# Attention block of an adaLN transformer layer: score and maxima products over 128 rows, zeroed padding rows, and the maxima product ahead of its score

## The chip, the cores and the metric

The kernel runs on one core of a Trainium2 chip. That core has a matrix engine (PE, with its weight loads shown as PEld), a vector engine (DVE), an activation engine (ACT), a general engine (POOL), a queue that issues transfers (SP), an on-chip memory of 128 partitions (rows), and 8 banks of accumulator memory, each 128 x 512 float32. The metric is the device time of one execution in microseconds (us); lower is better.

## The reference, cut to what matters

The input x is 2048 x 448. The block is a layer norm with modulation, attention with 16 heads of width 28, a residual, then a second layer norm with a gated MLP. Only the attention part is touched:

```
qkv = (x @ wqkv) -> q, k, v          # per head: 2048 x 28
scores = einsum("bhqd,bhkd->bhqk", q, k) * (28 ** -0.5)
p = softmax(scores, axis=-1)
o = einsum("bhqk,bhkd->bhqd", p, v)
```

## The kernel before, in words

**Split operands.** q and k are each kept as a high part and a low remainder, so that one product of 3 x 28 = 84 rows gives high·high + high·low + low·high. For each head there is a `kst` and a `qst` tile of 128 partitions x 2048 columns; three of each exist, and head h uses number h % 3. `load_head` (L343) fills rows 0 to 83 of both by six transfers from a scratch tensor in device memory.

**Two products for each score.** The softmax needs each query's maximum before the exponentials. So every block of scores is made twice. `m_mm` (L396) makes a 128-query x 512-key block with rows 0 to 83, and DVE reduces it to row maxima (L404). When a head's maxima are complete, `m_fin` (L412) transposes them, negates them, splits them in two and writes them by two transfers into rows 84 and 85 of `qst`. `s_mm` (L427) later makes a 128-key x 512-query block with rows 0 to 85: rows 84 and 85 of `kst` hold ones, so this product subtracts the maximum, and ACT takes the exponential (L434) into a tile `P`.

**The loop.** A unit is one block of 128 keys (for scores) or of 128 queries (for maxima); there are 16 x 16 = 256 units. In unit u the loop (L572) issues four score products of unit u and four maxima products of unit u + 20, alternating, score first. After every second unit it issues the eight value products of two units (`pv_mm`, L441), each 32 columns wide, four side by side, recorded as two passes each: 16 records. I call the 16 score and maxima products and the 16 records after them a **period**. There are 116 periods that hold pairs; the last units have scores only.

**What sets the order.** The order on each engine is written out by hand. Score and maxima blocks take their bank from one pool of 7 (`bank`, L161). Which earlier block's bank a product gets, and so whose release it waits for, is fixed when the program is built. A score block's bank is released by ACT's exponential, a maxima block's by DVE's reduction. Transfers go through SP in the order in which they are written.

**Before the loop.** The first 80 maxima products stand between the matrix products of `qk_unit` (L280), which make the last q and k columns. The `kst` and `qst` tiles come into being at g == 3 (L336), ahead of the last value products (L271). There POOL writes ones into rows 64 to 85 of `kst` tiles 0 and 1 (L346), and during `qk_unit` those of tile 2 (L569).

Of the kernel before, what the change touches and what calls it, by code (L numbers as in the profile page):

```python
# [8 lines left out]
F32 = mybir.dt.float32  # L9
# [24 lines left out]
def tile_adaln_mha_gmlp(ctx, tc, x, wqkv, wo, w_in, w_spT, b_sp, w_out, cT, w_mod, out):  # L34
    nc = tc.nc
    ctx.enter_context(tc.manual_schedule())
    pe, dve, act, pool, sp = nc.tensor, nc.vector, nc.scalar, nc.gpsimd, nc.sync
# [51 lines left out]
    def weight_part(dst, i, raw, hi_eng, lo_eng, zero=True):  # L89

        n = raw.shape[-1]
        h = dst[:, i if i < 3 else 6, 0:n]
        if hi_eng is act:
            act.activation(h, raw, AF.Copy)
        else:
            hi_eng.tensor_copy(h, raw)
        if i < 3:
            sub(lo_eng, dst[:, 3 + i, 0:n], raw, h)
        else:
            sub(lo_eng, dst[0:64, 7, 0:n], raw[0:64], h[0:64])  # L100
            if zero:
                pool.memset(dst[64:128, 7, 0:n].bitcast(F32), 0.0)
# [6 lines left out]
    def ln_transpose(xns, full_pool, dsts, scol, bcol, engs, los=(pool,) * 4, mid=None, after=None):  # L109

        tps = []
        for c in range(4):
            tp = bank("tp")
            tps.append(tp)
            for t in range(4):
                pe.transpose(tp[:, t * 128 : (t + 1) * 128], xns[t][:, c * 128 : (c + 1) * 128], ident)  # L116
        if mid:
            mid()
        for c in (0, 2, 1, 3):
            tp = tps[c]  # L120
            f = full_pool.tile([128, 512], F32, name="hfull")
            if engs[c] is act:
                act.activation(f, tp, AF.Identity, scale=scol[:, c : c + 1], bias=bcol[:, c : c + 1])
            else:
                engs[c].tensor_scalar(
                    out=f, in0=tp, scalar1=scol[:, c : c + 1], scalar2=bcol[:, c : c + 1], op0=ALU.mult, op1=ALU.add
                )
            hi = dsts[:, c if c < 3 else 6, :]
            if engs[c] is act:
                act.activation(hi, f, AF.Copy)  # L130
            else:
                engs[c].tensor_copy(hi, f)
            if c < 3:
                sub(los[c], dsts[:, 3 + c, :], f, hi)
            else:
                sub(los[c], hi[64:128], f[64:128], hi[64:128])
            if after:
                after(c)
# [22 lines left out]
    def bank(name):  # L161
        return ring.tile([128, 512], F32, name=name, tag="s")

    def load_mod(pair, eng):
        for k in range(4):
            wms[pair, k] = e1.tile([112, 2, D], F32, name="wm", bufs=4)
            eng.dma_start(wms[pair, k], w_mod[:, pair, k])

    def load_x(g, eng):
        xg = e1.tile([128, 4, D], F32, name="xg")  # L170
        for t0, t1 in ((0, 1), (1, 2), (2, 4)) if g == 0 else ((0, 4),):
            eng.dma_start(xg[:, t0:t1, :], x[g, :, t0:t1])
        for t in range(4):
            xts[4 * g + t] = xg[:, t, :]
# [91 lines left out]
    def v_tiles(*kts):  # L266
        pvs = [bank("pv") for _ in kts]
        for j, (a, b) in enumerate(STEPS):
            for kt, pv in zip(kts, pvs):
                g, t = divmod(kt, 4)  # L270
                pe.matmul(pv[:, :D], hT[g][:, a, t * 128 : (t + 1) * 128], wv[:, b, :], start=j == 0, stop=j == NST - 1)  # L271
        for kt, pv in zip(kts, pvs):
            dve.tensor_copy(V[:, kt, :, 0:DH], pv[:, :D].rearrange("p (h d) -> p h d", d=DH))

    def qk_unit(m, g, mid=None):
        pq = bank("pq")
        for j, (a, b) in enumerate(STEPS):
            if mid and j in mid:
                mid[j]()
            pe.matmul(pq, wqk[:, b, m * 128 : (m + 1) * 128], hT[g][:, a, :], start=j == 0, stop=j == NST - 1)  # L280
        f = stage.tile([128, 512], F32, name="qf")
        act.activation(f, pq, AF.Copy)  # L282
        hi = stage.tile([128, 512], F32R, name="qh")
        act.activation(hi, f, AF.Copy)
        lo = stage2.tile([128, 512], F32R, name="ql")
        sub(pool, lo, f, hi)
        for i, t in enumerate((hi, lo)):
            sp.dma_start(qk_scr[i][m * 128 : (m + 1) * 128, g * 512 : (g + 1) * 512], t.bitcast(F32))
# [42 lines left out]
    for g in range(NG):  # L331
        if g + 2 < NG:
            load_x(g + 2, sp)
        if g in (0, 2):
            load_mod(1 + g // 2, sp)
        if g == 3:  # L336
            early.close()
            stk = att.enter_context(tc.tile_pool(name="stk", bufs=1))
            kq = [[stk.tile([128, S], F32R, name=f"{n}st{i}") for n in "kq"] for i in range(3)]
            kst, qst = [a[0] for a in kq], [a[1] for a in kq]  # L340
            npool = att.enter_context(tc.tile_pool(name="npool", bufs=2))

            def load_head(h, c0=0, c1=S):  # L343
                k, q = kst[h % 3], qst[h % 3]
                if h < 2 and c0 == 0:
                    pool.memset(k[64:86, :].bitcast(F32), 1.0)  # L346
                for r0, i in ((0, 0), (56, 1), (28, 0)):
                    sp.dma_start(k[r0 : r0 + 28, c0:c1].bitcast(F32), qk_scr[i][D + h * DH : D + (h + 1) * DH, c0:c1])
                for r0, i in ((0, 0), (28, 1), (56, 0)):
                    sp.dma_start(q[r0 : r0 + 28, c0:c1].bitcast(F32), qk_scr[i][h * DH : (h + 1) * DH, c0:c1])  # L350

            load_head(0, 0, 1536)
            for m in (0, 3):
                qk_unit(m, g)
            load_head(0, 1536, S)
        if g == 0:
            v_tiles(0, 1)
            v_tiles(2)
        else:
            v_tiles(4 * g)  # L360
            v_tiles(4 * g + 1)
        if g == 0:
            for i in range(4):
                weight_part(wqk, i, raws.pop(("qk", i)), act, (dve, pool)[i % 2], False)
        if g + 1 < NG:
            ln_transpose(xns, e1, hT[g + 1], cols["ca"], cols["sa"], (act,) * 4)
        if g + 2 < NG:
            ln_stats(g + 2)
            xns = ln_norm(g + 2)
        if g > 0:  # L370
            v_tiles(4 * g + 2)
        else:
            pool.memset(V[:, :, :, DH:32], 1.0)
        v_tiles(4 * g + 3)
        if g == 2:
            mod_bc("ga", accs[1][:, 0, :])
            mod_col(("sb", accs[1][:, 1, :], 0.0))
        if g < 3:
            for m in (0, 3):
                qk_unit(m, g)  # L380
        if g in (1, 2):
            for k in range(4):
                mod_acc(g, k)
# [12 lines left out]
    def m_mm(j, kb):  # L396
        h, t = divmod(j, NT)
        mt = bank("mt")
        pe.matmul(  # L399
            mt, qst[h % 3][0:84, t * 128 : (t + 1) * 128], kst[h % 3][0:84, kb * 512 : (kb + 1) * 512], start=True, stop=True  # L400
        )
        if h not in pms:
            pms[h] = npool.tile([128, NT, 4], F32, name="pm")
        dve.tensor_reduce(out=pms[h][:, t, kb : kb + 1], in_=mt, axis=AX.X, op=ALU.max)  # L404
# [22 lines left out]
    def s_mm(u, qb):  # L427
        h, kt = divmod(u, NT)
        st = bank("st_ps")
        pe.matmul(st, kst[h % 3][0:86, kt * 128 : (kt + 1) * 128], qst[h % 3][0:86, qb * 512 : (qb + 1) * 512], start=True, stop=True)  # L430
        if qb % 2 == 0:
            ptiles[u, -1] = ppool.tile([128, 2, 512], F32, name="P")
        p = ptiles[u, -1][:, qb % 2, :]
        act.activation(p, st, AF.Exp, scale=SCALE)  # L434
        ptiles[u, qb] = p
# [129 lines left out]
                        fn(*a)  # L565

    for i, (m, g) in enumerate((m, g) for m in (4, 1, 5, 2, 6) for g in range(NG)):
        if i == 4:
            pool.memset(kst[2][64:86, :].bitcast(F32), 1.0)  # L569
        qk_unit(m, g, {j: m_first for j in (1, 4, 7, 10)})  # L570

    for u in range(NU + 1):  # L572
        for fn, a in events.pop(u, []):
            fn(*a)
        j = u + LEAD
        for qb in range(4 if u < NU else 0):
            s_mm(u, qb)
            if j < NU:
                m_mm(j, qb)
        if u % 2 == 0 and u > 0:  # L580
            pv_mm(u - 2)
            pv_mm(u - 1)
        for fn, a in late.pop(u, []):
            fn(*a)
# [109 lines left out]
    h = H - 1  # L694
# [203 lines left out]
    for tb in range(NG):  # L898
        nj = 3 if tb == NG - 1 else 2
        for st in range(NT - nj):  # L900
# [8 lines left out]
            if tb > 0 and 1 <= st < 13:  # L909
                t, part = 4 * (tb - 1) + (st - 1) // 3, (st - 1) % 3  # L910
# [54 lines left out]
```

## Time and profile before

| What | Value |
|---|---|
| median of 3 runs | 1462.51 us |
| profiled execution, its own time | 1460.85 us |
| span of its instructions | 1459.1 us |
| granted clock of the matrix engine, mean | 0.997 |
| PE busy | 1436.4 us (98%) |
| DVE busy | 881.3 us (60%) |
| ACT busy | 732.4 us (50%) |
| POOL busy | 276.3 us (19%) |
| score and maxima products | 1024 each |

The profile is of one execution. A matrix product's recorded time covers its way through the array, so consecutive ones overlap, and the step from one start to the next is what a product costs. A share of busy time says little here for the same reason; the timeline, which gives starts, says more. The `x1` or `x8` at the end of a timeline line is the number of instructions that were merged into it.

### The profile page before, as it was taken

The numbers are of one execution on the slowest core, as the hardware profiler recorded it, in microseconds if no ns is written. First come the engines' busy times: TensorE is split into PE (matmuls) and PEld (weight loads), VectorE is DVE, ScalarE is ACT, GpSimd is POOL, SyncE is SP. The second block draws the span as 40 slices with busy tenths as digits, with TensorE's granted clock in tenths as the row PEclk, the third lists the DMA queues.
The fourth block names the chain that finished last, engine by engine and source line by source line (L and its number), as shares of the span: only waits on it lengthen the run. The fifth ranks groups of instructions, "written<-read, shape, count | busy, mean of one in ns | idle before, by whom it ended". The sixth has DMA issues, their size and how long they took to land.

```text
span 1459.1 us, 19621 instructions
## 1 busy us (share of the span) xinstructions
PE 1436.4 (98%) x7314; PEld 1017.5 (70%) x7314; DVE 881.3 (60%) x1458; ACT 732.4 (50%) x1390; POOL 276.3 (19%) x255
## 2 busy tenths in 40 slices
PE   6999999999999999999999999999999999999999
PEld 5887755555555555555555556888988888888887
DVE  6557888888888888888888832921542411414114
ACT  3523576777677767777776786452432211211111
POOL 6734200000002021001000022100663400302002
PEclk9999999999999999999999999999999999999999
DMA  7564401221022211222132003432003322323223
GB/s 216 149 173 152 139 11 43 53 51 42 15 52 53 53 38 42 53 51 53 32 76 53 10 19 124 155 120 94 14 23 97 121 76 67 108 64 100 84 69 108
DMA packets 56131, 111.23 MB, mean 76 GB/s; under 512 B 11900, under 2 KB 22780, under 8 KB 53516
## 3 DMA queue, kind: packets, MB, share of 16 engines
q1 hardware_dynamic: 55910, 109.81, 25.9%
q8 instruction: 57, 0.93, 0.3%
q14 instruction: 38, 0.31, 0.1%
q10 hardware_dynamic: 126, 0.17, 0.0%
HBM read 75.89 MB, written 29.48 MB: 72 GB/s over the span
## 4 chain that ended last, share of the span: by engine, by line
PE 94%; DVE 3%; DMA 2%; issue 1%; SPq 0%; ACT 0%; POOL 0%; DVEq 0%; ACTq 0%
PE st_ps L430 18%; PE mt L399 16%; PE o_ps L445 16%; PE acc L848 6%; PE acc L850 6%; PE acc L849 6%; PE pq L280 5%; PE z_ps L802 5%; PE z_ps L736 5%; PE pv L271 2%; PE y_ps L889 2%; PE y_ps L888 2%; PE y_ps L890 2%; PE tp L116 1%; PE wo_ps L618 1%
## 5 line engine op out<-in xcount | busy, mean ns | idle before, releaser
L404 DVE TENSOR_REDUCE pm<-mt 128x1 f32<-128x512 f32 x1024 | 632.3, 683 | 120.6 <-PE mt L399 120.2
L434 ACT ACTIVATE P<-st_ps 128x512 f32<-128x512 f32 x1024 | 514.4, 621 | 153.4 <-PE st_ps L430 153.0
L430 PE MATMUL st_ps<-qst,kst 86*128 86x512 f32 x1024 | 410.6, 412 | 0.0
L399 PE MATMUL mt<-kst,qst 84*128 84x512 f32 x1024 | 405.7, 396 | 0.3 <-DVE pm L404 0.3
L430 PEld LDWEIGHTS st_ps<-qst,kst 86*128 86x128 f32 x1024 | 193.1, 189 | 145.2 <-issue 82.1
L445 PE MATMUL o_ps<-P,V 128*32 128x512 f32 x2048 | 247.5, 599 | 0.0
L399 PEld LDWEIGHTS mt<-kst,qst 84*128 84x128 f32 x1024 | 195.1, 190 | 37.1 <-DVE pm L404 0.7
L83 DVE TENSOR_TENSOR wsp_l<-raw_sp,wsp_h 128x512 fp32r<-128x512 f32 x64 | 50.8, 796 | 189.4 <-ACT wsp_h L785 189.4
L785 ACT ACTIVATE wsp_h<-raw_sp 128x512 fp32r<-128x512 f32 x64 | 40.2, 631 | 232.1 <-DMA raw_sp<-in_w_spT_dram 191.1
L445 PEld LDWEIGHTS o_ps<-P,V 128*32 128x32 f32 x2048 | 54.2, 109 | 123.4 <-issue 116.1
L83 POOL TENSOR_TENSOR heapF<-u,heapD 128x512 fp32r<-128x512 f32 x27 | 44.6, 1684 | 256.8 <-ACT heapD L867 256.8
L848 PE MATMUL acc<-wsp_h,heapD 128*128 128x512 f32 x224 | 87.7, 392 | 1.3 <-DVE u L865 1.3
L850 PE MATMUL acc<-wsp_h,heapD 128*128 128x512 f32 x224 | 87.5, 390 | 0.0
L849 PE MATMUL acc<-wsp_l,heapD 128*128 128x512 f32 x224 | 87.4, 390 | 0.0
L471 POOL TENSOR_TENSOR osb<-osb,rb 128x512 f32<-128x512 f32 x15 | 19.2, 1277 | 355.3 <-DMA rb<-r_scr 263.8
L280 PE MATMUL pq<-heapD 128*128 128x512 f32 x196 | 64.6, 407 | 0.0
L83 POOL TENSOR_TENSOR nl<-nf,nh 16x128 fp32r<-16x128 f32 x16 | 7.2, 449 | 278.9 <-issue 147.5
L893 DVE TENSOR_TENSOR x2t<-x2t,y_ps 128x448 f32<-128x448 f32 x12 | 7.4, 621 | 72.9 <-PE y_ps L890 72.9
L282 ACT ACTIVATE qf<-pq 128x512 f32<-128x512 f32 x28 | 16.7, 597 | 69.0 <-PE pq L280 69.0
L848 PEld LDWEIGHTS acc<-wsp_h,heapD 128*128 128x128 f32 x224 | 42.1, 188 | 10.5 <-DVE u L865 2.3
L850 PEld LDWEIGHTS acc<-wsp_h,heapD 128*128 128x128 f32 x224 | 42.1, 188 | 8.9
L849 PEld LDWEIGHTS acc<-wsp_l,heapD 128*128 128x128 f32 x224 | 42.1, 188 | 8.2
(162 smaller groups left out, 1753.8 us busy)
## 6 DMA issues: line engine op xcount, KB each, us to landing
raw_sp<-in_w_spT_dram SPq DMA_DIRECT2D x64, 256.0 KB
kst<-qk_scr SPq DMA_DIRECT2D x45, 224.0 KB
qst<-qk_scr SPq DMA_DIRECT2D x45, 224.0 KB
qk_scr<-qh SPq DMA_DIRECT2D x28, 256.0 KB
qk_scr<-ql SPq DMA_DIRECT2D x28, 256.0 KB
z_scr<-z1t SPq DMA_DIRECT2D x28, 256.0 KB
z<-z_scr SPq DMA_DIRECT2D x28, 256.0 KB
wm<-in_w_mod_dram SPq DMA_DIRECT2D x12, 392.0 KB
```

Of the source, the lines that this page charges most:

```text
L83: eng.tensor_tensor(out=dst, in0=a, in1=hi.bitcast(F32), op=ALU.subtract)
L280: pe.matmul(pq, wqk[:, b, m * 128 : (m + 1) * 128], hT[g][:, a, :], start=j == 0, stop=j == NST - 1)
L399: pe.matmul(mt, qst[h % 3][0:84, t * 128 : (t + 1) * 128], kst[h % 3][0:84, kb * 512 : (kb + 1) * 512], start=True, stop=True)
L404: dve.tensor_reduce(out=pms[h][:, t, kb : kb + 1], in_=mt, axis=AX.X, op=ALU.max)
L430: pe.matmul(st, kst[h % 3][0:86, kt * 128 : (kt + 1) * 128], qst[h % 3][0:86, qb * 512 : (qb + 1) * 512], start=True, stop=True)
L434: act.activation(p, st, AF.Exp, scale=SCALE)
L445: pe.matmul(otile[h][32 * qb : 32 * qb + 32, :], V[:, kt, h, :], ptiles.pop((u, qb)), start=kt == 0, stop=kt == NT - 1)
L736: pe.matmul(ps_t, w1[:, b, f * 128 : (f + 1) * 128], h2T[g][:, a, :], start=j == 0, stop=j == NST - 1)
L802: pe.matmul(ps_t[:, :D], h2T[g][:, a, tt * 128 : (tt + 1) * 128], w2[:, b, hf * D : (hf + 1) * D], start=j == 0, stop=j == NST - 1)
L848: pe.matmul(acc[f], z2[st][:, 0, fs], hi, start=st == 0, stop=False)
L849: pe.matmul(acc[f], z2[st][:, 0, fs], lo, start=False, stop=False)
L850: pe.matmul(acc[f], z2[st][:, 1, fs], hi, start=False, stop=st == NT - 1)
```

## The change

The change has four parts.

- **128 rows.** `m_mm` and `s_mm` read all 128 rows of `kst` and `qst` instead of 84 and 86.
- **Zeros.** A new function `pads` writes zeros into rows 64 to 127 of each `kst` tile on DVE, zeros into rows 64 to 127 of each `qst` tile (tile 0 on DVE, tiles 1 and 2 on POOL), and then the ones into rows 64 to 85 of `kst` on POOL. Tile 0 is done where the tiles come into being, tiles 1 and 2 after two value tiles; the three former writes of ones go.
- **Clearing the old maxima.** The maxima product now also reads rows 84 and 85 of `qst`, where ones in `kst` meet them. `load_head` therefore starts with one more transfer for each head from 3 on, which copies the zeros of rows 86 and 87 over the maxima that the tile's former head left.
- **Order.** In each pair of the loop the maxima product is issued ahead of the score product.

```diff
+            def pads(i, eng):
+                dve.memset(kst[i][64:128, :].bitcast(F32), 0.0)
+                eng.memset(qst[i][64:128, :].bitcast(F32), 0.0)
+                pool.memset(kst[i][64:86, :].bitcast(F32), 1.0)
+
+            pads(0, dve)
+
             def load_head(h, c0=0, c1=S):
                 k, q = kst[h % 3], qst[h % 3]
-                if h < 2 and c0 == 0:
-                    pool.memset(k[64:86, :].bitcast(F32), 1.0)
+                if h > 2:
+                    sp.dma_start(q[84:86, :].bitcast(F32), q[86:88, :].bitcast(F32))
...
             v_tiles(4 * g)
             v_tiles(4 * g + 1)
+        if g == 3:
+            pads(1, pool)
+            pads(2, pool)
...
-            mt, qst[h % 3][0:84, t * 128 : (t + 1) * 128], kst[h % 3][0:84, kb * 512 : (kb + 1) * 512], start=True, stop=True
+            mt, qst[h % 3][:, t * 128 : (t + 1) * 128], kst[h % 3][:, kb * 512 : (kb + 1) * 512], start=True, stop=True
...
-        pe.matmul(st, kst[h % 3][0:86, kt * 128 : (kt + 1) * 128], qst[h % 3][0:86, qb * 512 : (qb + 1) * 512], start=True, stop=True)
+        pe.matmul(st, kst[h % 3][:, kt * 128 : (kt + 1) * 128], qst[h % 3][:, qb * 512 : (qb + 1) * 512], start=True, stop=True)
...
-        if i == 4:
-            pool.memset(kst[2][64:86, :].bitcast(F32), 1.0)
...
         for qb in range(4 if u < NU else 0):
-            s_mm(u, qb)
             if j < NU:
                 m_mm(j, qb)
+            s_mm(u, qb)
```

## The prediction

> **What bounds the kernel now.** I read the list of costliest groups first.
>
> ```profile
> L404 DVE TENSOR_REDUCE pm<-mt 128x1 f32<-128x512 f32 x1024 | 632.3, 683 | 120.6 <-PE mt L399 120.2
> L434 ACT ACTIVATE P<-st_ps 128x512 f32<-128x512 f32 x1024 | 514.4, 621 | 153.4 <-PE st_ps L430 153.0
> L430 PE MATMUL st_ps<-qst,kst 86*128 86x512 f32 x1024 | 410.6, 412 | 0.0
> L399 PE MATMUL mt<-kst,qst 84*128 84x512 f32 x1024 | 405.7, 396 | 0.3 <-DVE pm L404 0.3
> ```
>
> DVE and ACT both wait for PE, and PE's products hardly wait. So in the loop PE's issue steps set the time. The timeline of one period (starts in the first column) gives these steps.
>
> ```profile
> 313.68 0.19 PEld L430 LDWEIGHTS st_ps<-qst,kst 86*128 86x128 f32 x1 [0.84 <-issue]
> 313.68 0.50 PE L430 MATMUL st_ps<-qst,kst 86*128 86x512 f32 x1
> 314.02 0.40 PE L399 MATMUL mt<-kst,qst 84*128 84x512 f32 x1
> ...
> 314.22 4.04 ACT L434 ACTIVATE P<-st_ps 128x512 f32<-128x512 f32 x8 [1.69 <-PE st_ps L430]
> 314.26 0.40 PE L430 MATMUL st_ps<-qst,kst 86*128 86x512 f32 x1
> ...
> 314.46 2.48 DVE L404 TENSOR_REDUCE pm<-mt 128x1 f32<-128x512 f32 x4 [0.92 <-PE mt L399]
> ...
> 317.30 0.39 PE L399 MATMUL mt<-kst,qst 84*128 84x512 f32 x1
> ...
> 317.62 1.92 PE L445 MATMUL o_ps<-P,V 128*32 128x512 f32 x16
> ```
>
> From 314.02 to 317.30 there are 14 steps: 3.28 / 14 = 0.234 us each. The first step is 0.34, since after the value products the weight load isn't ahead; the first score really starts 0.11 after its load, at 313.79. The next period begins at 319.47, 5.79 later. Over the 116 periods with pairs the trace has 5.82 on average.
>
> ACT starts 0.43 after its first score starts. Eight activations take 4.04, the last itself about 0.65: (4.04 - 0.65) / 7 = 0.485 from start to start. DVE: (2.48 - 0.68) / 3 = 0.60. ACT's 0.485 is slower than the 0.467 in which a pair is issued, so ACT falls behind within each period and catches up during the value products, 1.69 idle before the next. This decides below.
>
> **Part 1, 128 rows.** The trace has long rows of 128-row products with the same 512 columns.
>
> ```profile
> 1201.42 0.39 PE L848 MATMUL acc<-wsp_h,heapD 128*128 128x512 f32 x1
> 1201.65 0.39 PE L849 MATMUL acc<-wsp_l,heapD 128*128 128x512 f32 x1
> 1201.87 0.39 PE L850 MATMUL acc<-wsp_h,heapD 128*128 128x512 f32 x1
> ```
> ```profile
> 995.63 10.59 PE L736 MATMUL z_ps<-heap,heapA 128*128 128x512 f32 x46
> ```
>
> (10.59 - 0.39) / 45 = 0.2267 us a step, 0.0066 below the 0.2333 of the score and maxima products. Is it the rows, or that each of these products waits for a bank and signals? In `qk_unit` before the maxima products come (74 to 84 us) the 128-row products step at 0.227, waits between units included. Once one 84-row product stands after every three or four (95 to 100 us), every step is 0.231 to 0.238, also between two 128-row products. Around 1000 us DVE or ACT at work changes nothing. So I take the rows as the cause and 0.227 for the new step. The bounds are 0.227 and 0.234; a loss I exclude, as no long run of 128-row products is slower.
>
> The Trainium skill speaks against a gain: "TensorE: Matmul & The Clock Gate", section "Why this matters for your kernels", says that a product with a small contraction takes the same time as one of 128 rows. By that the sum is rival B's; the two rates above disagree with it, though they come from different lines.
>
> Saved if nothing else changed: 15 steps x 0.0066 = 0.10 a period, x 116 = 11.5 us; in `qk_unit` 300 products (80 + 20 units x 11) x 0.0064 = 1.9; where scores stand alone (10 blocks, step 0.231) 0.3. Sum 13.7 us.
>
> **Part 2, the order.** It moves no instruction to another engine, but which bank release each product waits for changes. I took the waits from both programs as built and number a period's products 0 to 15.
>
> Before, product 14 (a score) waits in most periods for the activation of product 8, the fifth score. Counted from product 0: that activation starts at 0.43 + 4 x 0.485 = 2.37, ends 0.62 later (L434's mean) at 2.99; the load follows a release by 0.05 (a reduction that ended at 305.30 let a load start at 305.35), and the product follows its load by 0.11: 3.15. By the steps alone it is due at 14 x 0.2333 = 3.27. No wait, by 0.12.
>
> After, product 14 is a maxima product and waits for the activation of product 9, again the fifth score, but the first score now starts one step later: 0.227 + 3.15 = 3.38. By the steps it is due at 14 x 0.227 = 3.18. It waits **0.20 us**. Behind it in PE's queue stand the last score and the value products, so the whole period moves. Net of the 0.10 saved: +0.10.
>
> So it is five times in the eight periods of a head. I carried the same durations through the other three. One, where product 14 waits for an older maxima block, has no wait: -0.10. The two after a head's maxima transpose (which takes a bank from the same pool) wait already in the trace (periods of 5.94 and 5.83) and get 0.08 and 0.13 longer. Carried through the program of before, the same rows give 5.78 and 5.94, near the trace. A head: 5 x 0.10 + 0.08 + 0.13 - 0.10 = 0.61, x 14.5 heads (116 periods / 8) = **+8.8 us**.
>
> DVE gains: its first block comes one step earlier. It isn't late: eight reductions of 0.60 are 4.8 in a period of 5.8.
>
> **Part 3, zeros and ones.**
>
> ```profile
> 0.82 0.17 DVE L52 MEMSET ones<- 128x128 f32 x1 [0.82 <-PEq L953]
> 0.93 0.06 DVE L54 MEMSET mhalf<- 128x4 f32 x1
> ```
> ```profile
> 82.17 1.80 POOL L346 MEMSET kst<- 22x2048 f32 x1
> ```
>
> POOL's write of 2048 columns takes 1.80, so 1.8 for its new ones. On DVE 124 columns more cost about 0.10, so 2048 cost some 1.75. Tile 0 (two on DVE, then POOL's ones) comes at about 79 to 84 us; DVE is idle from 78.6 to 86.7 and POOL writes its ones at 82.17 anyway. Tiles 1 and 2: 3.5 on DVE between the value copies of 88.96 and 91.20, which makes two copies up to 1.9 late; seven banks cover that. On POOL four writes, 7.2, from 87.2 on; it then has nothing to do until 100.1. The head's loads on SP wait for the scratch tensor until 84.2 and, for tile 1, issue at 96.5. I take 0; with this cover gone it would be tile 0's 5.3.
>
> **Part 4, the clearing transfer.** 13 transfers of 16 KB, first of each head's loads on SP, where such an issue takes 0.38. It waits for the former head's last score, as the loads behind it do. These loads are issued ten units (29 us) before their first maxima product, and no wait in the loop names a transfer on PE. Cost 0, at most those 13 x 0.38 = 5 us on SP, hidden.
>
> **The sum.** +8.8 - 1.9 - 0.3 = +6.6 us. On the profiled execution's 1460.85 that is 1467.5; the median is 1.7 above that execution, so I forecast **1469.1**, +0.5%. About 2% is what a measurement of this kernel can tell from no change.
>
> **Rivals.**
> - B, rows are free: the step stays 0.2333. Nothing is saved, and product 14 comes at 0.233 + 3.15 = 3.38 against 3.27: +0.115. A head: 5 x 0.115 + 0.09 + 0.13 = 0.80, x 14.5 = 11.5, so 1474. For it: every score and maxima product has its own wait and signal, those at 1000 us do not. Against: the 84-row products spoil the steps of their 128-row neighbours.
> - C, the other side: the activation's release comes early enough and the rows' gain stays whole. It decides at 0.20: product 14's load would have to find its bank free at 3.18 - 0.11 = 3.07 instead of 3.27, as with steps of ACT of 0.435. For it: ACT's steps vary between 0.477 and 0.494. Against: none is that short. 1462.5 - 13.7 = 1449.
> - D, neither a gain nor a wait: 1462.5.
> - E, weight loads no longer run ahead. The first step of a period shows the price: 0.34 instead of 0.23, 0.105 for each of 15 x 116 steps, +183, so 1645. Against: at L848 to L850, with 128 rows, the steps hold no load. The Trainium skill has such a rule, "TensorE: Matmul & The Clock Gate", section "Part 3: Packing small matmuls": a load overlaps a running product only where the row groups differ; the 0.227 steps contradict it.
>
> **How the numbers follow.** My case 0.58, B 0.20, C 0.10, D 0.04, a setup that shows or waits that spread 0.07, E 0.01. My case alone holds 1465 to 1473 (ACT's step of 0.477 or 0.494 moves the wait by 0.03, 2.4 us). The range goes up to B with the setup's 5.3, 1479, and down to a release 0.15 earlier than worked out (0.15 x 5 x 14.5 = 11), 1457, which holds D; C and the slowest are left out. Faster by over 2%: 0.02, slower by over 2%: 0.04, within: 0.94.
>
> **What would show it.** Steps of 0.227 between maxima and score products in most of a period; then one long step, 0.38 to 0.43, before product 14, with the weight load of `mt` waiting for ACT's `P` (9.4 us in all before, for `st_ps`), and a period near 5.9. Steps of 0.233 throughout show B; a period near 5.7 without the long step shows C. SP and POOL should show no new wait ahead of the first maxima product at 95.2. The forecast fails if the banks are released by other times than these, or if the steps between 128-row products that each wait and signal are neither of the two rates.

## The result and the profile after

The changed kernel takes 1474.2 us (median), the kernel before 1462.3: a ratio of 1.0087, 95% interval 1.0069 to 1.0105. One execution of the kernel before, at 3635.2 us, is left out of the ratio, so the ratio is not exactly the quotient of these medians. The change makes the kernel slower by 0.7 to 1.05%: less than the 2% that the prediction names, but the whole interval lies above 1. The forecast was 1469.1, +0.5%, and the time lies inside its range of 1457 to 1479.

The profiled execution after has a span of 1474.0 us, 15.0 more than before. By the first and last products of each stage in the two timelines it divides like this:

| Stage | before | after | difference |
|---|---|---|---|
| start to the first maxima product | 95.2 | 99.5 | +4.3 |
| from there to the first score (`qk_unit` with maxima products) | 70.4 | 68.8 | -1.6 |
| first score to the last value product (the loop) | 727.2 | 740.0 | +12.8 |
| the rest | 566.2 | 565.7 | -0.5 |

The 4.3 us at the start belong to this one execution. There DVE's longest wait for input rows was 9.6 us instead of 4.4, ahead of anything the change touches. Of the kernels below with the same setup, one begins its maxima products at 94.9, and one whose DVE waited 9.7 us begins them at 99.1. The loop is where the time came from.

The list of costliest groups of the changed kernel, for the lines that answer to those shown of before:

```profile
L415 DVE TENSOR_REDUCE pm<-mt 128x1 f32<-128x512 f32 x1024 | 631.4, 680 | 132.4 <-PE mt L410 132.1
L445 ACT ACTIVATE P<-st_ps 128x512 f32<-128x512 f32 x1024 | 512.9, 629 | 169.6 <-PE st_ps L441 168.2
L410 PE MATMUL mt<-kst,qst 128*128 128x512 f32 x1024 | 424.0, 414 | 0.3 <-DVE pm L415 0.3
L441 PE MATMUL st_ps<-qst,kst 128*128 128x512 f32 x1024 | 395.1, 397 | 0.0
```

The same instructions, all with 128 rows, and both DVE and ACT sit idle for PE longer than before (132 and 170 us against 121 and 153). PE itself shows next to no idle time, because the recorded times of its products overlap: below, product 13 is still recorded as running, to 339.91, when the late load of product 14 begins at 339.83. The load shows the wait. This is one ordinary period in the timeline of the changed kernel:

```profile
336.40 0.19 PEld L410 LDWEIGHTS mt<-kst,qst 128*128 128x128 f32 x1 [0.84 <-issue]
336.40 0.50 PE L410 MATMUL mt<-kst,qst 128*128 128x512 f32 x1
...
336.73 0.39 PE L441 MATMUL st_ps<-qst,kst 128*128 128x512 f32 x1
...
337.22 4.03 ACT L445 ACTIVATE P<-st_ps 128x512 f32<-128x512 f32 x8 [1.93 <-PE st_ps L441]
...
339.28 0.39 PE L410 MATMUL mt<-kst,qst 128*128 128x512 f32 x1
...
339.51 0.40 PE L441 MATMUL st_ps<-qst,kst 128*128 128x512 f32 x1
339.83 0.19 PEld L410 LDWEIGHTS mt<-kst,qst 128*128 128x128 f32 x1 [0.30 <-ACT P L445]
339.83 0.50 PE L410 MATMUL mt<-kst,qst 128*128 128x512 f32 x1
...
340.17 0.40 PE L441 MATMUL st_ps<-qst,kst 128*128 128x512 f32 x1
...
340.49 1.92 PE L456 MATMUL o_ps<-P,V 128*32 128x512 f32 x16
...
342.35 0.50 PE L410 MATMUL mt<-kst,qst 128*128 128x512 f32 x1
```

From product 1 (336.73) to product 13 (339.51) there are 12 steps of 2.78 / 12 = 0.232 us. Then the weight load of product 14 waits for the activation and begins at 339.83. The product really starts 0.11 later, at 339.94, 0.43 after product 13, so it lost 0.20. The period lasts 342.35 - 336.40 = 5.95 us, where an ordinary one lasted 5.77 to 5.81, 5.80 on average. Over all 116 periods the mean went from 5.818 to 5.932.

The list of waits shows the same in total. Its columns are the time, the number of waits and the longest. First the largest wait of a load for ACT before, then the one after:

```profile
PEld st_ps L430 <- ACT P L434: 9.4, 39, 0.4
```
```profile
PEld mt L410 <- ACT P L445: 34.8, 98, 0.8
```

Before, a maxima product's load waited 0.7 us in all for `P`.

### The profile page after: what moved, and what is told of

The parts are those of the page before. It is cut to its first block, busy times and chain, and to the rows that moved or that the text cites. A ratio compares the mean times of both kernels' runs of the same rounds, so it can differ in the third digit from the quotient of the medians.

```text
span 1474.0 us, 19620 instructions
## 1 busy us (share of the span) xinstructions
PE 1448.4 (98%) x7314; PEld 1008.6 (68%) x7314; DVE 887.4 (60%) x1462; ACT 732.4 (50%) x1390; POOL 282.2 (19%) x257
## 4 chain that ended last, share of the span: by engine, by line
PE 92%; DMA 3%; POOL 2%; DVE 1%; issue 1%; SPq 1%; ACT 0%; DVEq 0%; ACTq 0%; POOLq 0%
PE mt L410 19%; PE st_ps L441 16%; PE o_ps L456 16%; PE acc L858 6%; PE acc L859 6%; PE acc L857 6%; PE z_ps L811 5%; PE z_ps L745 5%; PE pq L280 4%; PE wo_ps L627 2%; PE y_ps L898 2%; PE y_ps L897 2%; PE y_ps L899 2%; DMA raw_sp<-in_w_spT_dram 1%; DMA raw<-in_wqkv_dram 1%
## 5 line engine op out<-in xcount | busy, mean ns | idle before, releaser
L410 PE MATMUL mt<-kst,qst 128*128 128x512 f32 x1024 | 424.0, 414 | 0.3 <-DVE pm L415 0.3
L441 PE MATMUL st_ps<-qst,kst 128*128 128x512 f32 x1024 | 395.1, 397 | 0.0
L410 PEld LDWEIGHTS mt<-kst,qst 128*128 128x128 f32 x1024 | 192.1, 188 | 143.3 <-issue 77.3
L441 PEld LDWEIGHTS st_ps<-qst,kst 128*128 128x128 f32 x1024 | 191.6, 188 | 61.7 <-issue 7.5
```

What stands on the lines that cost most here:

```text
L410: pe.matmul(mt, qst[h % 3][:, t * 128 : (t + 1) * 128], kst[h % 3][:, kb * 512 : (kb + 1) * 512], start=True, stop=True)
L441: pe.matmul(st, kst[h % 3][:, kt * 128 : (kt + 1) * 128], qst[h % 3][:, qb * 512 : (qb + 1) * 512], start=True, stop=True)
```

## Experiments

Theory 1 is the prediction's: the new order makes product 14 wait for the bank of the fifth score, the 128 rows save a little on each step, and the setup is hidden. Theory 2 puts the loss on the 128-row products. Theory 3 puts it on the setup and the clearing transfers.

### The order alone

```diff
         for qb in range(4 if u < NU else 0):
-            s_mm(u, qb)
             if j < NU:
                 m_mm(j, qb)
+            s_mm(u, qb)
```

> Only the order of each pair is changed; the products keep 84 and 86 rows, and the writes of ones stay as before. Theory 1 (the bank of the fifth score): product 14 of a period waits for the fifth activation, 3.38 us after product 0 against 3.27 due, so about +0.11 us in five of eight periods and about as much more around a head's maxima transpose; ordinary periods of 5.89 to 5.91 us, two long steps before and after product 14, about +11 us, ratio 1.006 to 1.009. Theory 2 (the 128-row products and what fills them are the loss, the order is free): periods as before, 5.78 to 5.80, ratio 0.999 to 1.001.

Measured: 1476.4 us, ratio 1.0100 (1.0085 to 1.0115). The loop takes 740.8 us, as in the changed kernel. The timeline of its PE shows products 12, 13 and 14 of a period:

```profile
339.06 0.40 PE L399 MATMUL mt<-kst,qst 84*128 84x512 f32 x1
339.30 0.39 PE L430 MATMUL st_ps<-qst,kst 86*128 86x512 f32 x1
339.58 0.50 PE L399 MATMUL mt<-kst,qst 84*128 84x512 f32 x1
```

The load of the last of these starts with the product, at 339.58, so the product starts at 339.69, 0.39 after the one before. Ordinary periods last 5.96 us, +0.17, more than the +0.11 expected, and the ratio is above the 1.006 to 1.009 expected. The trace shows where the other 0.06 comes from: ACT takes the first score 0.49 us after its start, as in the changed kernel, and not 0.43. The whole loss is here: the order makes it, without any of the other parts.

### The rows alone

The changed kernel with the former order:

```diff
         for qb in range(4 if u < NU else 0):
+            s_mm(u, qb)
             if j < NU:
                 m_mm(j, qb)
-            s_mm(u, qb)
```

> 128 rows with the zeros and the clearing transfer, but score first as before. Theory 1: no wait at product 14; the steps fall to 0.231 for the first seven products of a period and 0.227 behind them where no load is late, so periods of 5.72 to 5.76 us instead of 5.79, and 2 us less ahead of the loop; 1453 to 1458, ratio 0.994 to 0.998. Theory 2: the loss of the whole change stays here, ratio 1.005 to 1.009. If the rows do nothing at all: ratio 0.999 to 1.001.

Measured: 1454.3 us, ratio 0.9946 (0.9932 to 0.9961). **This kernel beats both.** Ordinary periods last 5.73 us and the mean period 5.775. In the middle of a period:

```profile
323.23 0.39 PE L410 MATMUL mt<-kst,qst 128*128 128x512 f32 x1
323.46 0.39 PE L441 MATMUL st_ps<-qst,kst 128*128 128x512 f32 x1
...
324.59 0.39 PE L410 MATMUL mt<-kst,qst 128*128 128x512 f32 x1
```

Six steps lie between the first and the last of these: (324.59 - 323.23) / 6 = 0.227 a step. Theory 2 falls. But not all steps are like this. After a period's first step they run 236, 228, 232 and 231 ns, sometimes with one or two more of this kind, before they stay at 227; that is reached at the sixth or seventh product. Where a load has waited even a little, the next steps swing in the same way. The mean of the steps below 0.25 is 0.2304 here, 0.2312 in the changed kernel, and 0.2341 before.

### The setup alone

The changed kernel with the former order and with 84 and 86 rows again:

```diff
-            mt, qst[h % 3][:, ...], kst[h % 3][:, ...]
+            mt, qst[h % 3][0:84, ...], kst[h % 3][0:84, ...]
...
-        pe.matmul(st, kst[h % 3][:, ...], qst[h % 3][:, ...]
+        pe.matmul(st, kst[h % 3][0:86, ...], qst[h % 3][0:86, ...]
```

> Zeros, ones and the clearing transfer of the change, but products of 84 and 86 rows and score first. Theory 1: hidden, ratio 0.999 to 1.001, the first maxima product at 95 to 97 us, periods as before. Theory 3 (the setup or the 13 transfers hold something up): 3 to 6 us more, ratio 1.002 to 1.004, seen as a later first maxima product or as long periods where the clearing transfers are issued.

Measured: 1461.4 us, ratio 1.0002 (0.9991 to 1.0014); first maxima product at 94.9 us, mean period 5.816. Theory 3 falls: zeros, ones and the 13 transfers cost nothing that can be measured (at most 2 us, by the interval).

### Shorter activations in the changed kernel

If product 14 waits for the fifth activation, a shorter activation must take the wait away although nothing on PE changes.

```diff
-            ptiles[u, -1] = ppool.tile([128, 2, 512], F32, name="P")
+            ptiles[u, -1] = pst[(2 * u + qb // 2) % 6]    # six fixed tiles, filled with ones
...
-        act.activation(p, st, AF.Exp, scale=SCALE)
+        act.activation(p[:, 0:384], st[:, 0:384], AF.Exp, scale=SCALE)
```

> The changed kernel with shorter activations: the exponential is taken of 384 of the 512 columns of each score block; the other 128 columns of six fixed P tiles hold ones, so that part of the softmax is left out. Nothing changes on the matrix engine. Theory 1: an activation step falls from 0.485 to about 0.37 us, the fifth is over before product 14 is due, the long steps there vanish and ordinary periods fall from 5.95 to 5.74 to 5.78 us; 1452 to 1458, ratio 0.993 to 0.998. If what product 14 waits for is not the activation but a reduction or the matrix engine itself: periods stay at 5.95 us, 1470 to 1475.

Measured: 1452.0 us, ratio 0.9935 (0.9919 to 0.9951). A period in its timeline, with seven of its eight activations and the last products:

```profile
317.65 3.29 ACT L448 ACTIVATE P<-st_ps 128x384 f32<-128x384 f32 x7 [1.97 <-PE st_ps L444]
...
319.96 0.39 PE L444 MATMUL st_ps<-qst,kst 128*128 128x512 f32 x1
320.19 0.39 PE L413 MATMUL mt<-kst,qst 128*128 128x512 f32 x1
320.42 0.40 PE L444 MATMUL st_ps<-qst,kst 128*128 128x512 f32 x1
```

Products 13, 14 and 15 follow each other at 0.23. Ordinary periods fall from 5.95 to 5.73 us, as long as with the rows alone: there the order costs nothing once ACT is quicker. One part of the expectation missed. An activation lasts 0.49 us instead of 0.62, but its step falls only to (3.29 - 0.49) / 6 = 0.47, not to 0.37, since ACT now keeps up with PE and waits for each score.

The same edit with 448 columns shows how close it is:

> The changed kernel with exponentials of 448 of the 512 columns (128 of the 1024 columns of each P tile hold ones instead; that part of the softmax is left out). Theory 1: the activation's own time falls by about 0.05 us and its step below the 0.463 us of a pair, so the fifth score's bank comes free 3.1 to 3.15 us after product 0, against a load due at 3.13: the wait shrinks from 0.20 us to less than 0.04 and ordinary periods fall from 5.95 to 5.73 to 5.78. If the release isn't what is waited for, periods stay at 5.95.

Measured, in a single execution: ordinary periods of 5.73 us, 1453.4 us. An activation lasts 0.54 us, and an eighth off its columns is enough.

### Which row counts make a step long

The prediction took 84 and 86 rows as too few. Three kernels on top of the one with the rows alone ask what it is about them. Only the upper row bound in the two products differs: 96 and 96 rows, 86 and 86, and 128 for maxima with 96 for scores.

> As the kernel with 128 rows, the zeros and score first, but both products read 96 rows, three whole groups of 32. If what slows the 84- and 86-row products is a group that is filled in part: settled steps of 0.227 us as with 128 rows, ordinary periods of 5.73, ratio 0.994 to 0.996. If it is any count below 128: settled steps of 0.233, periods of 5.78 to 5.80, ratio 0.999 to 1.001.

> Zeros, clearing transfer and score first as in the kernel with 128 rows, but both products read the same 86 rows. If a step is long because two products in succession read different numbers of rows (84 after 86): settled steps of 0.227 us in the loop as with 96 and 128 rows, ordinary periods of 5.71 to 5.78, and 0.233 ahead of the loop, where 86-row products stand between those of 128 rows; ratio 0.996 to 0.998. If a group of 32 rows that is filled in part makes it long: 0.233 in the loop too, periods of 5.78 to 5.81, ratio 0.999 to 1.001.

> The same with maxima products of 128 rows and score products of 96, both whole groups of 32, in alternation. If different row counts in succession make the step long: 0.233 us in the loop, periods of 5.78 to 5.81, but 0.227 ahead of the loop, where the maxima products have the 128 rows of their neighbours, 2 us less in all; ratio 0.998 to 1.000. If whole groups are what counts: 0.227 in the loop too, periods of 5.71 to 5.78, ratio 0.994 to 0.997.

Measured, each ratio beside executions of the kernel before that ran with it. The step beside the products of `qk_unit` is the mean of those below 0.25 us; the settled step in the loop is the one that long stretches of a period stay at:

| maxima rows, score rows | step beside the 128-row products of `qk_unit` | settled step in the loop | loop, us | ratio to before (95%) |
|---|---|---|---|---|
| 84, 86 (before) | 0.2332 | 0.233 | 727.2 | 1 |
| 86, 86 | 0.2332 | 0.227 | 723.5 | 0.9985 (0.9973 to 0.9997) |
| 96, 96 | 0.2332 | 0.227 | 723.3 | 0.9971 (0.9961 to 0.9981) |
| 128, 96 | 0.2269 | 0.233 | 727.3 | 0.9992 (0.9982 to 1.0002) |
| 128, 128 | 0.2269 | 0.227 | 722.2 | 0.9946 (0.9932 to 0.9961) |

From the timeline with 86 and 86 rows:

```profile
329.79 0.39 PE L441 MATMUL st_ps<-qst,kst 86*128 86x512 f32 x1
330.01 0.39 PE L410 MATMUL mt<-kst,qst 86*128 86x512 f32 x1
...
330.92 0.39 PE L410 MATMUL mt<-kst,qst 86*128 86x512 f32 x1
```

and with 128 and 96 rows:

```profile
325.02 0.39 PE L410 MATMUL mt<-kst,qst 128*128 128x512 f32 x1
325.25 0.40 PE L441 MATMUL st_ps<-qst,kst 96*128 96x512 f32 x1
...
326.19 0.40 PE L441 MATMUL st_ps<-qst,kst 96*128 96x512 f32 x1
```

Five steps each: 1.13 / 5 = 0.226 with 86 equal rows, 1.17 / 5 = 0.234 with 128 and 96. Steps are long where the products in succession read **different numbers of rows**. Among 86, 96 and 128 it does not matter how many they read, nor whether groups of 32 are full. Ahead of the loop the neighbours have 128 rows, so there only a 128-row maxima product keeps the short step. That each of these products waits and signals doesn't matter either: the 86-row ones do too.

Two of the expected ratios were missed. With 96 equal rows the kernel is at 0.9971, not 0.994 to 0.996, for the most part because its long steps of 0.2332 in `qk_unit` stayed (1.9 us, or 0.0013); with 86 equal rows it is at 0.9985, just above 0.996 to 0.998, with an interval that reaches into that range.

### The transpose ahead of the value products

Each head has two long periods also with the rows alone, 5.94 and 5.82 us. This kernel moves one step of it:

```diff
+        for fn, a in late.pop(u, []):
+            fn(*a)
         if u % 2 == 0 and u > 0:
             pv_mm(u - 2)
             pv_mm(u - 1)
-        for fn, a in late.pop(u, []):
-            fn(*a)
```

> As the kernel with 128 rows, the zeros and score first, and the maxima transpose of a head is issued ahead of the value products of its unit instead of behind them, so that its bank comes free during them. If the two long periods of each head (5.94 and 5.83 us with 128 rows and score first) come from the bank that the transpose takes at the start of a period: the second falls to 5.73, the first to 5.73 plus the transpose's own 0.1 to 0.23; 1.5 to 4.5 us less than with 128 rows and score first, ratio to the kernel before 0.991 to 0.994. If they come from something else around the head's end: unchanged, ratio 0.995.

```profile
336.39 0.39 PE L410 MATMUL mt<-kst,qst 128*128 128x512 f32 x1
336.62 0.27 PE L426 MATMUL mtp<-ident,mxv 128*16 128x128 f32 x1
336.82 1.92 PE L456 MATMUL o_ps<-P,V 128*32 128x512 f32 x16
```

The period with the transpose lasts 5.84 us and the next 5.73, as expected. But of the 116 periods 62 now last 5.74 to 5.79 us where 34 did, and 32 stay at 5.73 where 50 did; why is not shown. The mean period is 5.763 against 5.775. The ratio, 0.9960 (0.9946 to 0.9975), misses the 0.991 to 0.994 expected and is no better than with the rows alone. So the place of the transpose makes the second long period and 0.10 of the first; that its move gains time is not shown.

## Why the prediction was right or wrong

**Right: the sign, and the place.** Product 14 waits for the activation of the fifth score, as forecast. The order alone brings the whole loss, and shorter activations take it away: that is shown. In the trace of the changed kernel the load of product 14 begins 0.05 us after the end of the fifth activation in each of the 74 ordinary periods (all but the one with a transpose and the two behind it in each head).

**Luck: the 0.20 us of that wait.** It is the difference of two times, and both came later than worked out. The load was put at 3.27 us after product 0; in the period shown above it begins at 339.83 - (336.40 + 0.11) = 3.32. Without a wait the product was due at 3.18 by the forecast; a step of 0.23 behind product 13 it would have come at 3.23. Two errors of 0.05 leave the difference as it was.

**Mis-sized: when the bank of the fifth score comes free.** What makes a period longer is not the wait by itself but the time at which product 14 starts. Over the ordinary periods that was 3.28 us after product 0 before and is 3.44 now; the forecast had 3.27 and 3.38. The missing 0.06 lies in the first term of the chain on ACT. The prediction carried over the 0.43 us between a score's start and its activation; with the maxima product first it is 0.49. In the trace a wait instruction of 17 ns stands in ACT's own queue ahead of that activation in 87 of the 102 periods without a transpose, with 0.49 to 0.50 there, and in the other 15 it is missing, with 0.43 to 0.44. So an ordinary period got 0.16 longer, not 0.10. Over five periods of 14.5 heads that is 0.06 x 72.5 = 4.4 us, about as much as the forecast of the loop lacked: it had +8.8 - 0.3 = 8.5, against 12.8.

**Mis-sized too, but without weight here: the rows, 0.10 saved a period.** "15 steps x 0.0066" took the settled step of long rows of like products for every step. In the changed kernel the steps below 0.25 average 0.2312, 0.003 below before, so about 0.04 a period is saved. With the former order the rows save 0.06: ordinary periods of 5.74 on average instead of 5.80. A step first has to settle over six or seven products after each block of value products, and swings again after each load that waits a little. The steps after the break at 74.18 us in `qk_unit` (0.233, 0.231, then 0.227) hinted at it. But once product 14 has to wait, quicker steps ahead of it only lengthen the wait: with the order alone and steps of 0.2333 product 14 starts at 3.44 too, and the periods are as long.

**Wrong: "I take the rows as the cause".** The number was near for this change, since it makes both counts equal. The cause was not: with 96 or 86 equal rows the settled step is 0.227 too. The sign was in the view that I read. In `qk_unit` 84-row products spoilt the steps of their 128-row neighbours, which fits a change of the count at least as well as a count that is too low. The rule of the Trainium skill that rival B leaned on ("TensorE: Matmul & The Clock Gate", section "Why this matters for your kernels": a small contraction takes the time of a full one) agrees with the runs as long as the counts are equal: 0.227 with 86, 96 and 128 rows.

**The other periods of a head.** Forecast +0.08, +0.13 and -0.10. Measured: the one with the transpose 5.93 against 5.94, the next 5.95 to 5.96 against 5.83, the one without the wait 5.76 to 5.78 against 5.80. So -0.01, +0.13, -0.03. With 5 x 0.16 a head gains 0.89, x 14.5 = 12.9, and the loop has +12.8.

The +0.13 of the period after a transpose is DVE's, not ACT's. There the load of product 15, the last score, waits for a reduction. First the changed kernel, then the one with 384 columns, where it is the same:

```profile
263.05 0.19 PEld L441 LDWEIGHTS st_ps<-qst,kst 128*128 128x128 f32 x1 [0.39 <-DVE pm L415]
```
```profile
257.01 0.19 PEld L444 LDWEIGHTS st_ps<-qst,kst 128*128 128x128 f32 x1 [0.40 <-DVE pm L418]
```

It begins 0.05 us after the end of the fifth reduction of that period. That is why this period lasts 5.95 to 5.96 us with 384 and with 448 columns too. The prediction said that DVE isn't late, from its 4.8 us in a period of 5.8; that holds for the sum, but not for the bank that this one product gets.

**Right: `qk_unit`.** Forecast -1.9, measured -1.6, and the step is 0.2269 against 0.2332.

**Wrong, but small: the scores that stand alone**, forecast -0.3. Such a block lasts 3.92 us before and after. Its eight scores end where the steps begin to settle: after the first step they average 0.2315 before and 0.2302 after. What holds the block at 3.92 is not shown; with activations of 384 and 448 columns it lasts 3.89 and 3.92 by turns, so the activations are not much of it.

**Right: zeros, ones and clearing at 0.** The setup alone measures 1.0002. The clearing transfer takes 0.67 us on SP to issue, not 0.38, and stays hidden all the same.

**The range and the rivals.** The prediction's own case was to hold 1465 to 1473, and 1474.2 lies just above that; the range holds it because it reaches up to B with a setup that costs 5.3, and neither came about, so that it fell inside is in part luck. (Its lower end is 1 us further off than its sum: 1469.1 - 11 = 1458.) B's time, 1474, is the measured one, but its step of 0.2333 is not: it is the case of the order alone, which took 1476.4. C (the gain whole, no wait) did not come about; the kernel with the rows alone is what is left of it, at 1454 instead of 1449. For E, no run here shows a load that 128 rows keep from running ahead.

What is left open is why ACT's queue has the extra wait ahead of the first score in the new order, and why steps settle as they do.

## What to carry to other kernels

Where two consumers free the banks of one pool, the order in which their products are issued decides whose release comes too late: follow the slower consumer's chain from its first start to the product that gets its bank, and compare with the due time. The delay of that first start can itself change with the order. Here a start that came 0.23 us later, and 0.06 more until ACT took the score, turned a slack of 0.12 into a wait of 0.16 to 0.20. And let products that alternate on PE read the same number of rows: here the padding cost nothing that could be measured, and alternating counts cost 6 to 7 ns on each step.

## What the runs showed of the hardware that was not expected

- The step between products of 512 columns is 0.2267 us where successive products read the same number of rows (86, 96 or 128) and 0.2333 where the number changes (84 and 86, 128 and 96, 84, 86 or 96 beside 128), also for 128-row neighbours that do not change themselves.
- After a break the short step is reached only at the sixth or seventh product, by way of steps of 236, 228, 232 and 231 ns (128 rows, score first), so that the steps of a period average 0.2304 us and not 0.2267.
- An activation whose place in ACT's queue has a separate wait instruction ahead of it starts 0.49 us after its score, one without it 0.43 us (changed kernel, first score of a period).
